# A decode step on one core: an instruction stream with two empty blocks and a hinted jump, one weight load per row of W1, a plain load of Wq, and thirty small marker loads

## The chip, the cores and the metric

The kernel runs on one core of one Trainium2 chip. Its engines are TensorE (PE, with its weight loads shown apart as PEld), VectorE (DVE), ScalarE (ACT), GpSimd (POOL) and SyncE (SP). Sixteen DMA engines move data between the chip's memory (HBM) and the core's SBUF. The metric is the device time of one execution in microseconds, as the median of the runs shown.

## The reference

One token (a row x of 1024 values) passes through two branches, and the sum of both and x is the output. Everything is bf16 at the boundary.

```
xn = layernorm(x)
q  = xn @ wq                      # 1024 x 4096: 32 heads of 128
k, v = the last 4096 rows of the cache, 4 key/value heads, each used by 8 query heads
o  = softmax(q k^T / sqrt(128)) v
A  = o @ wo                       # 4096 x 1024
y  = layernorm(xn)
B  = gelu(y @ w1 + b1) @ w2 + b2  # 1024 x 3584 and 3584 x 1024
out = x + A + B
```

Nearly all of the data is used once: wq and wo have 8 MB each, w1 and w2 7 MB each, and the two windows of the cache 4 MB each, some 40 MB in all.

## The kernel before, in words

Every engine's program is written out by hand, with semaphores between them. Two engines issue loads: SP has one queue (q1 in the profile) with all the large ones, and ACT has another (q10) with x, b1 and b2 (lines 165 to 167). In q1 the order is W1 (one load of 128 rows of 57,344 bytes), Wq in two halves, the two key loads, the two value loads, W2, and Wo in four pieces of 20, 10, 1 and 1 chunks (`WO_CHUNKS`; a chunk is 2 KB on each of 128 partitions). W2 is written over W1, so SP waits for TensorE's mark "h" (line 364); Wo is written over Wq, so SP waits for "q" (line 366). The values wait for "b1" (line 362).

Wq's second half is loaded in a special way. The even partitions get their full rows (line 229) and the odd partitions get rows that lack the last `CUT` = 1024 columns (line 230). The 64 pieces of 2 KB that are missing come by four more loads of 16 rows each (line 233) into the tile `WX`, which lies where the probabilities `Pb` will later be. TensorE needs the matching 48 values of x for these pieces, so GpSimd gathers them (line 183), TensorE turns them (line 266), VectorE normalizes them (line 286), and four more matmuls use them (line 354). The holes in `WA` are multiplied by zeros (`XNZ7`, line 292). The loads at lines 229 to 233 wait for GpSimd to have cleared the holes (lines 169 and 170).

TensorE's program runs in this order: turning x, two sums for the layer norms, b1 into seven PSUM banks (line 315), y times W1 (line 324: 8 rows of 7 matmuls, each preceded by its own weight load of one column of y), xn times Wq (line 345: 64 matmuls, then the four of line 354), eight units of sixteen transposes of the keys (line 405), the scores (line 431), the turning of h (line 438), softmax with VectorE and ScalarE, probabilities times values (line 510), and the products with W2 and Wo (line 494). At its end ScalarE copies the result out of PSUM (line 547) and SP stores it (line 549).

Within one piece of the product with Wo, TensorE waits for that piece's load alone; the last piece, of one chunk, has four matmuls.

Of the kernel before, what the change touches and what calls it, by code (L numbers as in the profile page):

```python
# [5 lines left out]
ALU = mybir.AluOpType  # L6
ACTF = mybir.ActivationFunctionType
AX = mybir.AxisListType
# [11 lines left out]
KC = D // 128  # L20
NQ = HQ * DH
WQ_CHUNKS = [4, 4]
W1_CHUNKS = [8]
W2_CHUNKS = [28]
WO_CHUNKS = [20, 10, 1, 1]
KEEP_BUSY = [[512] * 5, [], [], []]
NPAIR = HKV // 2
PB = 2 * NBLK
CUT = 1024
B1W = 256  # L30
B1N = F // B1W
XS = 2
XROWS = 48
OUTSIDE = -1e30
# [15 lines left out]
def bass_parallel_sum__sliding_block_cached__mixer_channel_mlp__decode_kernel(  # L50
# [18 lines left out]
    pe, dve, act, pool, sp = nc.tensor, nc.vector, nc.scalar, nc.gpsimd, nc.sync  # L69

    def sems(name, n):
        return [nc.alloc_semaphore(f"{name}{i}") for i in range(n)]

    s_xrow, s_b1, s_b2, s_out = (nc.alloc_semaphore(n) for n in ("s_xrow", "s_b1", "s_b2", "s_out"))
    s_wq = sems("s_wq", len(WQ_CHUNKS))
    s_ex = nc.alloc_semaphore("s_ex")
    s_w1 = sems("s_w1", len(W1_CHUNKS))
# [6 lines left out]
    DVE = Track(nc, "S_DVE")  # L84
    ACT = Track(nc, "S_ACT")
    POOL = Track(nc, "S_POOL")

    def sb(name, shape, d):
        return nc.alloc_sbuf_tensor(name, shape, d)

    f32, bf16 = dt.float32, dt.bfloat16
    identb = sb("identb", [128, 128], bf16)
    identf = sb("identf", [128, 128], f32)
# [5 lines left out]
    oneb = sb("oneb", [128, 1], bf16)  # L99
    XBR = sb("XBR", [1, 2 * D], bf16)  # L100
    XT16 = sb("XT16", [128, 16], f32)
    msx = sb("msx", [128, 8], f32)
    XNT = sb("XNT", [128, 8], f32)
    XNTb = sb("XNTb", [128, 8], bf16)
    XNZ = sb("XNZ", [128, KC * 15], bf16)
    EVEN = sb("EVEN", [128, 1], f32)
    XNZ7 = sb("XNZ7", [128, 15], bf16)
    XPR = sb("XPR", [1, XS * XROWS], bf16)
    XEZ = sb("XEZ", [XROWS, XS * 15], bf16)
    YT16 = sb("YT16", [128, 16], f32)  # L110
# [14 lines left out]
    Pb = sb("Pb", [128, PB * HQ], bf16)  # L125
# [11 lines left out]
    WA = sb("WA", [128, KC * NQ], bf16)  # L137
    WX = Pb[0:XROWS, 0:XS * CUT]
    PS = nc.alloc_psum_tensor("PS", [128, 8 * 512], f32)
# [5 lines left out]
    wq_p = A_wq.rearrange("(p r) n -> p r n", r=KC)  # L145
    wq_runs = A_wq.rearrange("(p r) n -> p (r n)", r=KC)
    wq_x = A_wq.rearrange("(s h r e k) n -> k s h e r n", s=XS, h=2, r=4, e=4)[2 * KC - 1]
    w1_p = B_w1.rearrange("(p r) n -> p r n", r=KC)
    w2_p = B_w2.rearrange("(p c) n -> p c n", c=FC)
    wo_p = A_wo.rearrange("(p j) n -> p j n", j=32)  # L150
    out_rows = out.rearrange("b s (a n) -> (b s a) n", a=4)

    C = {}

    def load_rows(dst, src, chunks, width, semaphores):
        c0 = 0
        for j, n in enumerate(chunks):
            sp.dma_start(  # L158
                dst[:, c0 * width:(c0 + n) * width].rearrange("p (c n) -> p c n", c=n),
                src[:, c0:c0 + n, :],  # L160
            ).then_inc(semaphores[j], 16)
            c0 += n
# [5 lines left out]

    POOL.mark(pool.memset(WA[:, KC * NQ - CUT:KC * NQ], 0.0))
    C["hole"] = POOL.mark(pool.memset(WX, 0.0))  # L170
    POOL.mark(pool.memset(XPR[:, :], 0.0))
    C["oneb"] = POOL.mark(pool.memset(oneb[:, :], 1.0))
# [4 lines left out]
        out=identb[:, :], in_=identb[:, :], pattern=[[-1, 128]], compare_op=ALU.not_equal,  # L177
        fill=1.0, base=0, channel_multiplier=1))
    pool.wait_ge(s_xrow, 16)
    for i in range(XS):  # L180
        at = i * 2 * 16 * 2 * KC
        dst = XPR[0:1, i * XROWS:(i + 1) * XROWS].rearrange("o (g m) -> o g m", g=3)[:, 0:3:2, :]
        C["xpr"] = POOL.mark(pool.tensor_copy(
            dst.rearrange("o h (e r) -> o h e r", e=4),
            XBR[0:1, at + 2 * KC - 1:at + 2 * 16 * 2 * KC:2 * KC].rearrange("o (h r e) -> o h e r", h=2, e=4)))
    POOL.mark(pool.memset(identf[:, :], 0.0))
# [3 lines left out]
        fill=1.0, base=0, channel_multiplier=1))  # L190
    POOL.mark(pool.memset(XNZ[:, :], 0.0))
    POOL.mark(pool.memset(XNZ7[:, :], 0.0))
    C["xnz"] = POOL.mark(pool.memset(XEZ[:, :], 0.0))
    POOL.mark(pool.memset(E4[:, :], 0.0))
# [17 lines left out]
    at = PAR[:, :].rearrange("k (m g) -> k m g", g=2)  # L212
# [12 lines left out]
    load_rows(W1, w1_p, W1_CHUNKS, F, s_w1)  # L225
    load_rows(WA, wq_p, WQ_CHUNKS[:-1], NQ, s_wq)
    sp.wait_ge(POOL.sem, C["hole"])
    c0 = (KC - WQ_CHUNKS[-1]) * NQ
    sp.dma_start(WA[0:128:2, c0:KC * NQ], wq_runs[0:128:2, c0:KC * NQ]).then_inc(s_wq[-1], 16)
    sp.dma_start(WA[1:128:2, c0:KC * NQ - CUT], wq_runs[1:128:2, c0:KC * NQ - CUT]).then_inc(s_wq[-1], 16)  # L230
    for i in range(XS):
        for h in range(2):
            sp.dma_start(WX[32 * h:32 * h + 16, i * CUT:(i + 1) * CUT], wq_x[i, h, :, :, NQ - CUT:NQ]).then_inc(s_ex, 16)

# [10 lines left out]
    def stats(src, ms, veps):  # L245
# [10 lines left out]
            out=ms[:, 5:6], in0=ms[:, 3:4], scalar=EPS, in1=ms[:, 4:5], op0=ALU.add, op1=ALU.subtract))  # L256

    xt = PS[:, 7 * 512 + 16: 7 * 512 + 24]
    pe.wait_ge(POOL.sem, C["oneb"])
    pe.wait_ge(s_xrow, 16)  # L260
    for r in range(KC):
        last = pe.matmul(xt[:, r:r + 1], lhsT=XBR[0:1, r:D:KC], rhs=oneb[0:1, :])
    xe = PS[0:XROWS, 7 * 512 + 24: 7 * 512 + 24 + XS]
    pe.wait_ge(POOL.sem, C["xpr"])
    for i in range(XS):
        last = pe.matmul(xe[:, i:i + 1], lhsT=XPR[0:1, i * XROWS:(i + 1) * XROWS], rhs=oneb[0:1, :])
    C["xt"] = PE.mark(last)
# [15 lines left out]
    DVE.mark(dve.tensor_scalar(out=XNT[:, :], in0=XT16[:, 0:8], scalar1=msx[:, 2:3], scalar2=msx[:, 7:8],  # L283
                               op0=ALU.subtract, op1=ALU.mult))
    dve.wait_ge(POOL.sem, C["xnz"])
    DVE.mark(dve.tensor_scalar(out=XEZ[:, 7:XS * 15:15], in0=xe, scalar1=msx[0:XROWS, 2:3], scalar2=msx[0:XROWS, 7:8],
                               op0=ALU.subtract, op1=ALU.mult))
    C["even"] = DVE.mark(dve.tensor_reduce(out=EVEN[:, 0:1], in_=identf[:, 0:128:2], axis=AX.X, op=ALU.add))
    dve.wait_ge(DVE.sem, DVE.cnt)
    C["xn"] = DVE.mark(dve.tensor_copy(XNTb[:, :], XNT[:, :]))  # L290
    pool.wait_ge(DVE.sem, C["xn"])
    C["xnz7"] = POOL.mark(pool.tensor_tensor(out=XNZ7[:, 7:8], in0=XNTb[:, KC - 1:KC], in1=EVEN[:, 0:1], op=ALU.mult))
    dve.wait_ge(DVE.sem, DVE.cnt)
# [10 lines left out]
    act.wait_ge(ACT.sem, ACT.cnt)  # L304
    ACT.mark(act.activation(out=EXPW[:, 0:1], in_=msy[:, 6:7], func=ACTF.Exp))
    dve.wait_ge(ACT.sem, C["std2"])
    DVE.mark(dve.reciprocal(out=msy[:, 7:8], in_=msy[:, 6:7]))
# [12 lines left out]
    for j, n in enumerate(W1_CHUNKS):  # L320
        pe.wait_ge(s_w1[j], 16)
        for _ in range(n):
            for t in range(7):
                last = pe.matmul(  # L324
                    PS[0:1, t * 512:(t + 1) * 512], lhsT=YTb[:, k:k + 1],
                    rhs=W1[:, k * F + t * 512: k * F + (t + 1) * 512],
                    start=False, stop=(k == KC - 1))
            k += 1
    C["h"] = PE.mark(last)
# [7 lines left out]
    for j, n in enumerate(WQ_CHUNKS):  # L337
        pe.wait_ge(s_wq[j], 16 if j < len(WQ_CHUNKS) - 1 else 32)
        for _ in range(n):
            for t in range(8):  # L340
                cut = k == KC - 1 and (t + 1) * 512 > NQ - CUT
                if cut:
                    pe.wait_ge(POOL.sem, C["xnz7"])
                z = XNZ7[:, 7 - t:15 - t] if cut else XNZ[:, 15 * k + 7 - t:15 * k + 15 - t]
                pe.matmul(  # L345
                    PS[0:8, 7 * 512:8 * 512], lhsT=z,
                    rhs=WA[:, k * NQ + t * 512: k * NQ + (t + 1) * 512],
                    start=(k == 0 and t == 0), stop=False)
            k += 1
    pe.wait_ge(s_ex, 32 * XS)  # L350
    for i in range(XS):
        for t in range((NQ - CUT) // 512, 8):
            at = i * CUT + t * 512 - (NQ - CUT)
            last = pe.matmul(  # L354
                PS[0:8, 7 * 512:8 * 512], lhsT=XEZ[:, 15 * i + 7 - t:15 * i + 15 - t], rhs=WX[:, at:at + 512],
                start=False, stop=(i == XS - 1 and t == 7))
    C["q"] = PE.mark(last)
# [33 lines left out]
    for u in range(NUNIT):  # L391
# [11 lines left out]
        for bb in range(16):  # L403
            o = banks[bb // 8] * 1024 + (bb % 8) * 128
            last = pe.matmul(PSb[:, o:o + 128], lhsT=KT[:, col + bb * 128: col + (bb + 1) * 128],  # L405
                             rhs=identb[:, :], is_transpose=True)
        C["ktr"][u] = PE.mark(last)
        use_act = u not in (2, 5)
        dve.wait_ge(PE.sem, C["ktr"][u])
# [134 lines left out]
    C["fin"] = PE.mark(last)  # L544

    act.wait_ge(PE.sem, C["fin"])
    C["a_out"] = ACT.mark(act.activation(out=ORow[:, :], in_=PS[:, 6 * 512:6 * 512 + 256], func=ACTF.Copy))  # L547
# [33 lines left out]
```

## Time and profile before

| what | value |
|---|---|
| time, median of 3 runs | 100.78 us (100.48, 100.78, 100.81) |
| span of the profiled execution, first to last instruction | 99.4 us |
| own time of the profiled execution | not listed apart from the three runs; median less span is 1.4 us |
| TensorE busy | 69.6 us (70% of the span), 763 matmuls, mean granted clock 0.897 |
| weight loads | 763, 42.4 us busy, beside the matmuls |
| VectorE, ScalarE, GpSimd busy | 25.8, 12.8 and 9.0 us |
| moved by DMA | 39.96 MB, mean 402 GB/s |
| queue q1 | 1832 packets, 94.1% of 16 engines' span |

The page cuts the span into 40 slices of 2.48 us and gives each engine's busy share in tenths; the DMA row is the mean share of the 16 DMA engines. A queue's share of 94.1% says that the sixteen engines were occupied with q1's packets in 94.1% of the whole span, so that a slice at 9 is a slice in which the large loads ran without a hole. A third queue, q8, is called "instruction": the fetches of program code from memory, six in this execution, of 16,384 bytes each.

### The profile page before, as it was taken

The page shows a single profiled execution, that of the slowest core. Times are in us where ns is not written, and L with a number is a line of the kernel's source. Part 1 is how long each engine was busy: PE and PEld are TensorE (multiplying, and loading weights), DVE is VectorE, ACT ScalarE, POOL GpSimd, SP SyncE. Part 2 cuts the span into 40 slices and gives each one's busy share as a digit, 9 for nine tenths or more (in the row PEclk, how much of TensorE's full clock was granted, in tenths as well). Part 3 has the DMA queues.
Part 4 walks back from the last instruction along what each step waited for, and adds up shares of the span by engine and source line. Part 5 has one row for each costly group of instructions (what it writes and reads, how often), then busy time and mean ns, then how long its engine had stood idle before and what let it go on. Part 6 is the DMA issues. An engine that isn't in the chain of part 4 may idle for free.

```text
span 99.4 us, 1681 instructions
## 1 busy us (share of the span) xinstructions
PE 69.6 (70%) x763; PEld 42.4 (43%) x763; DVE 25.8 (26%) x50; ACT 12.8 (13%) x15; POOL 9.0 (9%) x30
## 2 busy tenths in 40 slices
PE   0230860089999999999999999722799995009961
PEld 0220300023434343434399869510567894008740
DVE  0058500000000090000078921867790040000000
ACT  0500240000000050000065730005200000000001
POOL 7989100000000000000000000000000000000000
PEclk9999999999999999999999999555557999855799
DMA  9988889999999999999999999998999899699930
GB/s 347 392 372 369 370 369 485 465 422 422 422 422 422 409 402 403 441 429 442 429 429 422 429 534 416 468 485 369 392 485 425 346 445 528 287 404 437 405 143 1
DMA packets 1870, 39.96 MB, mean 402 GB/s; under 512 B 244, under 2 KB 262, under 8 KB 584
## 3 DMA queue, kind: packets, MB, share of 16 engines
q1 hardware_dynamic: 1832, 39.85, 94.1%
q8 instruction: 6, 0.10, 0.4%
q10 hardware_dynamic: 32, 0.01, 0.0%
HBM read 39.86 MB, written 0.00 MB: 401 GB/s over the span
## 4 chain that ended last, share of the span: by engine, by line
DMA 65%; PE 31%; ACT 0%; SPq 0%; issue 0%
DMA WA<-in_A_wo_dram 46%; DMA W<-in_B_w_dram 19%; PE PS L324 15%; PE PS L345 14%; PE PS L494 2%; PE PS L354 1%; ACT ORow L547 0%; SPq L158 0%
## 5 line engine op out<-in xcount | busy, mean ns | idle before, releaser
L324 PE MATMUL PS<-W,YTb 128*1 128x512 bf16 x56 | 14.4, 425 | 6.2 <-DMA W<-in_B_w_dram 6.2
L345 PE MATMUL PS<-WA,XNZ 128*8 128x512 bf16 x64 | 14.0, 379 | 0.0
L324 PEld LDWEIGHTS PS<-W,YTb 128*1 128x1 bf16 x56 | 5.1, 91 | 16.0 <-issue 10.3
L510 PE MATMUL PS<-KV,Pb 128*32 128x256 bf16 x64 | 10.0, 333 | 1.2 <-ACT Pb L471 1.2
L494 PE MATMUL PS<-WA,OT 128*32 128x256 bf16 x128 | 5.6, 345 | 7.1 <-DMA WA<-in_A_wo_dram 7.1
L345 PEld LDWEIGHTS PS<-WA,XNZ 128*8 128x8 bf16 x64 | 5.6, 88 | 8.2
L510 PEld LDWEIGHTS PS<-KV,Pb 128*32 128x32 bf16 x64 | 7.4, 118 | 3.9 <-ACT Pb L471 1.7
L494 PEld LDWEIGHTS PS<-WA,OT 128*32 128x32 bf16 x128 | 4.5, 123 | 8.4 <-issue 6.3
L333 DVE CAST ROW<-PS 1x2048 bf16<-1x2048 f32 x1 | 2.3, 2279 | 22.2 <-PE PS L324 22.2
L417 ACT ACTIVATE KV<-PS 128x1024 bf16<-128x1024 bf16 x6 | 5.8, 1021 | 16.1 <-PE PS L405 16.1
L405 PE MATMUL PS<-identb,KV 128*128 128x128 bf16 x128 | 7.5, 219 | 0.0
L405 PEld LDWEIGHTS PS<-identb,KV 128*128 128x128 bf16 x128 | 7.2, 98 | 0.5 <-issue 0.4
L412 DVE COPY KV<-PS 128x1024 bf16<-128x1024 bf16 x10 | 6.4, 686 | 1.1 <-PE PS L405 1.1
L331 ACT ACTIVATE ROW<-PS 1x1536 bf16<-1x1536 f32 x1 | 1.4, 1440 | 21.2 <-PE PS L324 21.2
L359 DVE CAST Q<-PS 8x512 bf16<-8x512 f32 x1 | 0.7, 678 | 12.5 <-PE PS L354 12.5
L475 DVE TENSOR_REDUCE SUMP<-Pb 128x32 f32<-128x2048 bf16 x1 | 3.6, 3566 | 1.2 <-ACT Pb L471 1.2
L547 ACT ACTIVATE ORow<-PS 128x256 bf16<-128x256 f32 x1 | 0.4, 384 | 27.0 <-PE PS L494 27.0
L299 PE MATMUL PS<-YT,onesf 128*128 128x16 f32 x2 | 0.6, 383 | 4.2 <-DVE YT L297 4.2
L431 PEld LDWEIGHTS PS<-QT,KV 128*128 128x128 bf16 x128 | 3.3, 96 | 0.4 <-issue 0.4
L494 PE MATMUL PS<-W,GT 128*32 128x256 bf16 x112 | 3.4, 273 | 0.0
L431 PE MATMUL PS<-QT,KV 128*128 128x16 bf16 x128 | 3.4, 169 | 0.0
L442 DVE TENSOR_REDUCE MXP<-PS 128x32 f32<-128x2048 f32 x1 | 2.3, 2292 | 3.9 <-PE PS L431 3.9
(104 smaller groups left out, 48.8 us busy)
## 6 DMA issues: line engine op xcount, KB each, us to landing
W<-in_B_w_dram SPq DMA_DIRECT2D x2, 7168.0 KB, 31.0
WA<-in_A_wo_dram SPq DMA_DIRECT2D x1, 5120.0 KB, 40.0
WA<-in_A_wq_dram SPq DMA_DIRECT2D x1, 4096.0 KB, 28.6
KV<-in_A_k_cache_dram SPq DMA_DIRECT2D x2, 2048.0 KB, 40.2
KV<-in_A_v_cache_dram SPq DMA_DIRECT2D x2, 2048.0 KB, 43.6
WA<-in_A_wo_dram SPq DMA_DIRECT2D x1, 2560.0 KB, 45.7
WA<-in_A_wq_dram SPq DMA_DIRECT2D x1, 2048.0 KB, 31.2
WA<-in_A_wq_dram SPq DMA_DIRECT2D x1, 1920.0 KB, 36.7
```

Source lines behind the costliest of these rows:

```text
L324: last = pe.matmul(PS[0:1, t * 512:(t + 1) * 512], lhsT=YTb[:, k:k + 1], rhs=W1[:, k * F + t * 512: k * F + (t + 1) * 512], start=False, s ...
L331: C["a_hrow"] = ACT.mark(act.activation(out=Hrow[:, 0:1536], in_=PS[0:1, 0:1536], func=ACTF.Copy))
L333: C["d_hrow"] = DVE.mark(dve.tensor_copy(Hrow[:, 1536:F], PS[0:1, 1536:F]))
L345: pe.matmul(PS[0:8, 7 * 512:8 * 512], lhsT=z, rhs=WA[:, k * NQ + t * 512: k * NQ + (t + 1) * 512], start=(k == 0 and t == 0), stop=False)
L405: last = pe.matmul(PSb[:, o:o + 128], lhsT=KT[:, col + bb * 128: col + (bb + 1) * 128], rhs=identb[:, :], is_transpose=True)
L412: C["dkt"][u] = DVE.mark(dve.tensor_copy(KT[:, col + 1024 * s: col + 1024 * (s + 1)], PSb[:, bk * 1024:(bk + 1) * 1024]))
L417: C["akt"][u] = ACT.mark(act.activation(out=KT[:, col + 1024: col + 2048], in_=PSb[:, bk * 1024:(bk + 1) * 1024], func=ACTF.Copy))
L431: last = pe.matmul(PS[:, o:o + 2 * REP], lhsT=KT[:, (i * PB + b) * 128:(i * PB + b + 1) * 128], rhs=QT[:, i * 2 * REP:(i + 1) * 2 * REP], ...
L442: C["mxp"] = DVE.mark(dve.tensor_reduce(out=MXP[:, :], in_=PS[:, 0:2048].rearrange("p (b n) -> p n b", b=PB), axis=AX.X, op=ALU.max))
L475: C["sump"] = DVE.mark(dve.tensor_reduce(out=SUMP[:, :], in_=Pb[:, :].rearrange("p (b n) -> p n b", b=PB), axis=AX.X, op=ALU.add))
L494: ins = pe.matmul(acc(a), lhsT=vec[:, c:c + 32], rhs=weights[:, c * D + a * 256: c * D + (a + 1) * 256], start=False, stop=(c == stop_at))
L510: last = pe.matmul(PS[0:32, 4 * 512:4 * 512 + NPAIR * DH], lhsT=Pb[:, b * HQ:(b + 1) * HQ], rhs=V4[:, :, b, :], start=(b == 0), stop=(b == ...
```

## The change

The changed kernel does four things.

- Wq is loaded by two plain loads of 128 full rows. `CUT`, `WX`, `XPR`, `XEZ`, `XNZ7` and all that served them (three memsets, the gathers, six matmuls, three operations of VectorE, one of GpSimd, four loads, SP's wait) go.
- In the product with W1, the first matmul of each row loads the column of y, and the other six are issued as matmuls without a weight load (`again`).
- TensorE's first instruction is a branch-prefetch hint. After the fourth unit of key transposes its program has a branch that is never taken, a hinted jump to `L_far`, and then three alignments to 256 instructions, so that the third and the fourth block of 256 hold nothing that runs.
- ScalarE issues a series of fifteen small loads twice (`marks`): load n takes n rows of 2n values of x (4n bytes) to n partitions. The first series stands behind the operation of line 305, the second ahead of the final copy, and ScalarE waits for all of the first before the second and for all of the second before the copy.

```diff
+JUMP_AT = 363
-CUT = 1024
-XS = 2
-XROWS = 48
...
+    MK = sb("MK", [128, 240], bf16)
...
+    def again(out, lhsT, rhs, start, stop):
+        return pe.add_instruction(mybir.InstMatmult(
+            name=nc.get_next_instruction_name(), engine=pe.engine, ins=[pe.lower_ap(rhs), pe.lower_ap(lhsT)], outs=[pe.lower_ap(out)],
+            start_tensor_calc=start, stop_tensor_calc=stop, ldweights=False, tile_size=(128, 32), tile_position=(0, 0)))
...
+    def marks():
+        for n in range(1, 16):
+            act.dma_start(MK[0:n, n * (n - 1):n * (n + 1)],
+                          A_x.rearrange("b s (k n) -> (b s k) n", n=64)[0:n, 0:2 * n]).then_inc(s_mark, 16)
+
+    never = pe.alloc_register("never")
+    done = [72]
+
+    def count(n):
+        done[0] += n
+        if done[0] - n < JUMP_AT <= done[0]:
+            pe.br_lt(never, 0, on_true="L_gap", on_false="L_go")
+            nc.switch_bb("L_go", parent=None)
+            pe.br("L_far").branch_hint(C["hint"])
+            nc.switch_bb("L_gap", parent=None)
+            for _ in range(3):
+                pe.nop(hint="gap")
+                pe.addr_align(256, offset=0, max_nops=0)
+            pe.br("L_far")
+            nc.switch_bb("L_far", parent=None)
...
-    load_rows(WA, wq_p, WQ_CHUNKS[:-1], NQ, s_wq)
-    sp.wait_ge(POOL.sem, C["hole"])
-    c0 = (KC - WQ_CHUNKS[-1]) * NQ
-    sp.dma_start(WA[0:128:2, c0:KC * NQ], wq_runs[0:128:2, c0:KC * NQ]).then_inc(s_wq[-1], 16)
-    sp.dma_start(WA[1:128:2, c0:KC * NQ - CUT], wq_runs[1:128:2, c0:KC * NQ - CUT]).then_inc(s_wq[-1], 16)
-    for i in range(XS):
-        for h in range(2):
-            sp.dma_start(WX[32 * h:32 * h + 16, i * CUT:(i + 1) * CUT], wq_x[i, h, :, :, NQ - CUT:NQ]).then_inc(s_ex, 16)
+    load_rows(WA, wq_p, WQ_CHUNKS, NQ, s_wq)
...
+    C["hint"] = pe.mark_branch_hint_location()
+    pe.reg_mov(never, 0)
...
     ACT.mark(act.activation(out=EXPW[:, 0:1], in_=msy[:, 6:7], func=ACTF.Exp))
+    marks()
...
             for t in range(7):
-                last = pe.matmul(
+                put = pe.matmul if t == 0 else again
+                last = put(
                     PS[0:1, t * 512:(t + 1) * 512], lhsT=YTb[:, k:k + 1],
...
+            count(8)
...
+    act.wait_ge(s_mark, 16 * 15)
+    marks()
+    act.wait_ge(s_mark, 2 * 16 * 15)
     act.wait_ge(PE.sem, C["fin"])
```

More of the change, by code (lines that the diff above doesn't have):

```diff
@@ L72, in sems @@
         return [nc.alloc_semaphore(f"{name}{i}") for i in range(n)]
+    s_mark = nc.alloc_semaphore("s_mark")
     s_xrow, s_b1, s_b2, s_out = (nc.alloc_semaphore(n) for n in ("s_xrow", "s_b1", "s_b2", "s_out"))
     s_wq = sems("s_wq", len(WQ_CHUNKS))
-    s_ex = nc.alloc_semaphore("s_ex")
     s_w1 = sems("s_w1", len(W1_CHUNKS))
@@ L104, in bass_parallel_sum__sliding_block_cached__mixer_channel_mlp__decode_kernel @@
     XNTb = sb("XNTb", [128, 8], bf16)
+    MK = sb("MK", [128, 240], bf16)
     XNZ = sb("XNZ", [128, KC * 15], bf16)
[L106 to L109, printed above, removed]
     YT16 = sb("YT16", [128, 16], f32)
@@ L137, in bass_parallel_sum__sliding_block_cached__mixer_channel_mlp__decode_kernel @@
     WA = sb("WA", [128, KC * NQ], bf16)
-    WX = Pb[0:XROWS, 0:XS * CUT]
     PS = nc.alloc_psum_tensor("PS", [128, 8 * 512], f32)
@@ L145, in bass_parallel_sum__sliding_block_cached__mixer_channel_mlp__decode_kernel @@
     wq_p = A_wq.rearrange("(p r) n -> p r n", r=KC)
-    wq_runs = A_wq.rearrange("(p r) n -> p (r n)", r=KC)
-    wq_x = A_wq.rearrange("(s h r e k) n -> k s h e r n", s=XS, h=2, r=4, e=4)[2 * KC - 1]
     w1_p = B_w1.rearrange("(p r) n -> p r n", r=KC)
@@ L167, in bass_parallel_sum__sliding_block_cached__mixer_channel_mlp__decode_kernel @@
     act.dma_start(XBR[:, D:2 * D], b2_row).then_inc(s_b2, 16)
-    POOL.mark(pool.memset(WA[:, KC * NQ - CUT:KC * NQ], 0.0))
-    C["hole"] = POOL.mark(pool.memset(WX, 0.0))
-    POOL.mark(pool.memset(XPR[:, :], 0.0))
     C["oneb"] = POOL.mark(pool.memset(oneb[:, :], 1.0))
@@ L178, in bass_parallel_sum__sliding_block_cached__mixer_channel_mlp__decode_kernel @@
         fill=1.0, base=0, channel_multiplier=1))
-    pool.wait_ge(s_xrow, 16)
-    for i in range(XS):
[L181 to L185, printed above, removed]
     POOL.mark(pool.memset(identf[:, :], 0.0))
@@ L190, in bass_parallel_sum__sliding_block_cached__mixer_channel_mlp__decode_kernel @@
         fill=1.0, base=0, channel_multiplier=1))
-    POOL.mark(pool.memset(XNZ[:, :], 0.0))
-    POOL.mark(pool.memset(XNZ7[:, :], 0.0))
-    C["xnz"] = POOL.mark(pool.memset(XEZ[:, :], 0.0))
+    C["xnz"] = POOL.mark(pool.memset(XNZ[:, :], 0.0))
     POOL.mark(pool.memset(E4[:, :], 0.0))
@@ L225, in bass_parallel_sum__sliding_block_cached__mixer_channel_mlp__decode_kernel @@
     load_rows(W1, w1_p, W1_CHUNKS, F, s_w1)
-    load_rows(WA, wq_p, WQ_CHUNKS[:-1], NQ, s_wq)
-    sp.wait_ge(POOL.sem, C["hole"])
-    c0 = (KC - WQ_CHUNKS[-1]) * NQ
-    sp.dma_start(WA[0:128:2, c0:KC * NQ], wq_runs[0:128:2, c0:KC * NQ]).then_inc(s_wq[-1], 16)
-    sp.dma_start(WA[1:128:2, c0:KC * NQ - CUT], wq_runs[1:128:2, c0:KC * NQ - CUT]).then_inc(s_wq[-1], 16)
-    for i in range(XS):
-        for h in range(2):
-            sp.dma_start(WX[32 * h:32 * h + 16, i * CUT:(i + 1) * CUT], wq_x[i, h, :, :, NQ - CUT:NQ]).then_inc(s_ex, 16)
+    load_rows(WA, wq_p, WQ_CHUNKS, NQ, s_wq)
     def load_cache(dst, cache, semaphores):
@@ L262, in bass_parallel_sum__sliding_block_cached__mixer_channel_mlp__decode_kernel @@
         last = pe.matmul(xt[:, r:r + 1], lhsT=XBR[0:1, r:D:KC], rhs=oneb[0:1, :])
[L263 to L266, printed above, removed]
     C["xt"] = PE.mark(last)
@@ L284, in bass_parallel_sum__sliding_block_cached__mixer_channel_mlp__decode_kernel @@
                                op0=ALU.subtract, op1=ALU.mult))
+    dve.wait_ge(DVE.sem, DVE.cnt)
+    DVE.mark(dve.tensor_copy(XNTb[:, :], XNT[:, :]))
     dve.wait_ge(POOL.sem, C["xnz"])
[L286 to L292, printed above, removed]
     dve.wait_ge(DVE.sem, DVE.cnt)
@@ L337, in bass_parallel_sum__sliding_block_cached__mixer_channel_mlp__decode_kernel @@
     for j, n in enumerate(WQ_CHUNKS):
-        pe.wait_ge(s_wq[j], 16 if j < len(WQ_CHUNKS) - 1 else 32)
+        pe.wait_ge(s_wq[j], 16)
         for _ in range(n):
             for t in range(8):
[L341 to L346, printed above, removed]
+                last = pe.matmul(
+                    PS[0:8, 7 * 512:8 * 512], lhsT=XNZ[:, 15 * k + 7 - t:15 * k + 15 - t],
                     rhs=WA[:, k * NQ + t * 512: k * NQ + (t + 1) * 512],
-                    start=(k == 0 and t == 0), stop=False)
+                    start=(k == 0 and t == 0), stop=(k == KC - 1 and t == 7))
+                count(2)
             k += 1
[L350 to L356, printed above, removed]
     C["q"] = PE.mark(last)
@@ L407, in bass_parallel_sum__sliding_block_cached__mixer_channel_mlp__decode_kernel @@
         C["ktr"][u] = PE.mark(last)
+        count(32)
         use_act = u not in (2, 5)
```

## The prediction

> **What bounds the kernel now.** I read the chain of waits first, then the DMA queues, then the busy time by stage over the last microseconds, and last each load's sixteen completion writes.
>
> ```profile
> by line: DMA WA<-in_A_wo_dram 46.0%; DMA W<-in_B_w_dram 19.5%; PE PS L324 14.5%; PE PS L345 13.9%; PE PS L494 1.6%; PE PS L354 1.0%; ACT ORow L547 0.4%; SPq L158 0.3%; issue 0.3%
> ...
> 20.28 14.43 PE PS L324 x56
> 34.71 13.81 PE PS L345 x64
> 48.52 0.97 PE PS L354 x4
> 49.49 0.02 issue
> 49.51 0.34 SPq L158
> 49.85 0.04 issue
> 49.89 45.70 DMA WA<-in_A_wo_dram
> 95.59 0.04 issue
> 95.64 1.61 PE PS L494 x48
> ```
>
> The chain shows TensorE for 29 us between W1's load and Wo's. That is misleading: Wo is issued at 49.5 us because "q" is ready then, but it stands behind the values and W2 in a queue that never runs empty.
>
> ```profile
> DMA  9988889999999999999999999998999899699930
> ...
> q1 hardware_dynamic: 1832, 39.85, 94.1%
> q8 instruction: 6, 0.10, 0.4%
> ```
>
> 94.1% of 99.4 us is 93.5 us of packets on each of 16 engines, from 1.8 us to 96.4 us. So DMA is the bound from end to end: 39.85 MB at the 27.1 GB/s of one engine (a 57,344-byte packet takes 2.116 us) are 91.9 us. TensorE waits for Wo's first piece, and this is its slack:
>
> ```profile
> PE PS L494 <- DMA WA<-in_A_wo_dram: 7.1, 2, 6.2
> ```
>
> The end is set by the **slowest of the sixteen engines**. The table by stage gives PE, weight load, DVE, ACT, POOL, then the granted clock, the DMA share and GB/s:
>
> ```profile
> 94.50:95.00 0.50, 0.17 (x1) 0.00 (x0) 0.00 (x0) 0.00 (x0) 0.00 (x0) 1.00 0.47 176
> 95.00:95.50 0.50, 0.00 (x0) 0.00 (x0) 0.00 (x0) 0.00 (x0) 0.00 (x0) 1.00 0.59 225
> 95.50:96.00 0.50, 0.36 (x16) 0.36 (x20) 0.00 (x0) 0.00 (x0) 0.00 (x0) 1.00 0.52 197
> 96.00:96.50 0.50, 0.50 (x28) 0.49 (x20) 0.00 (x0) 0.00 (x0) 0.00 (x0) 1.00 0.12 45
> ```
>
> About half of the engines are still loading for 1.5 us after the other half have finished. The completion writes (us, sorted, from the trace) tell which work made them late:
>
> ```
> Wq, 1st half    all 16 within 29.32 to 29.88
> Wq, even rows   15 from 38.73 to 39.22, one at 40.83
> values, 2nd     10 from 58.31 to 58.80, six from 59.78 to 60.41
> W2              8 from 75.26 to 75.75, eight from 76.72 to 77.36
> Wo, 1st piece   7 from 87.41 to 87.87, nine from 88.85 to 89.48
> Wo, last piece  7 from 94.81 to 95.31; 96.25 96.32 96.42 96.56; 96.57 96.58 96.65 96.71 96.87
> ```
>
> The instruction fetches start at 36.59, 56.24, 64.49, 75.15, 85.86 and 96.75 us, and after each of the first five one more engine is late. Each fetch hit a *different* engine, by 1.55 us (39.27 expected, 40.83 seen): about 1.0 us in which it moves no data, and 0.5 us by which its next packet is stretched (a 30,720-byte packet takes 1.687 instead of 1.138 us). Four others are late since the pieces of line 233, whose completion writes come from four engines only: 16 pieces of 2 KB each, four in 0.337 us, about 1.3 us. So nine engines are late, and the last completion at 96.87 us is the first fetch's engine, which had also been the last of all before it. Four matmuls, the copy and the store then take 2.5 us.
>
> **The change part by part.**
>
> *Wq plain.* The 64 cut pieces come from all engines alike (4 rows each, 8 KB) and go to four. Undone, four engines get 24 KB less and twelve, the five late ones among them, 8 KB more: 8192 / 27.1 GB/s = **+0.30 us** on each fetch engine. This is the surest term. The operations that go (GpSimd's 1.8 and 0.95 us memsets, line 286, the 0.97 us of line 354) lie beside the loads of W1 and Wq: worth nothing, for the queue is full without them. SP no longer waits 2.3 us at line 229; the loads ahead of it last until 29 us, so nothing.
>
> *One weight load per row.* Line 324 needs 14.43 / 56 = 258 ns per matmul and line 345 216 ns. If the 48 matmuls without loads go at 216 ns, TensorE gains 48 x 42 ns = 2.0 us. Bounds: nothing to 2.0 us, and a loss if such a matmul were slower. Both are hidden, since W2 is issued at 34.7 us and its turn in the queue comes at 59 us. On the time: 0.
>
> *Jump and hint.* [...] Engines without a fetch end within 0.50 us of one another (94.81 to 95.31), and before the latest of them was hit. After: the same (0) or an earlier one (down to -0.30). I take **-0.1**. [...]
>
> The row for code fetches is 16 KB in 0.93 us, ahead of any need. [...]
>
> *Markers.* Load n has n rows, so 2 x 120 = 240 data packets and as many completion writes, at most 30 of each on one engine, 15 on the mean. (The b1 load of 14 rows made 14 packets and 14 writes.) Nearest rows: 9 ns for a 4-byte packet, 27 ns for 512 bytes, 17 ns for a completion write between the pieces of line 233. Lower bound 0: the b1 engines show no visible delay at W1's end. Upper: 30 x 44 = 1.32 us. I take 15 x 15 ns = **+0.2**, nearest to the 4-byte row. ScalarE issues fifteen at 0.43 to 0.85 us each: 6 to 13 us, from 13.6 us (next needed at 34.7) and from 70.2 us (next needed at 97.3), so hidden. The waits: behind the second stands only the final copy. A small load advances by one packet per packet of q1 (b2 needed from 2.7 to 13.7 us), so 30 steps from 70 us end near 95 us, within the loads. Cost 0; cover about 1 us.
>
> **Sum.** Last completion 96.87 + 0.30 - 0.1 + 0.2 = 97.3 us; span 99.4 + 0.4 = 99.8 us; with the 1.4 us between span and median, **101.2 us**. Bounds of the three terms: 100.8 to 102.4.
>
> **Rivals.**
>
> *Same engine twice.* If a block is fetched twice (hint early, pushed out, fetched again) or two blocks share an engine, that engine is late twice. For: only five distinct engines are known. Against: all five did differ. Price: 0.6 us (16 KB at packet speed) to 1.55 us more, 101.8 to 102.8; it decides once one engine has two fetches before 96 us.
>
> [...]
>
> *Fewer or cheaper fetches.* If a fetch costs only the 1.0 us, or code comes before the loads start, the last is 96.3 us: 100.2. Against: all five measured about 1.55.
>
> [...]
>
> **Numbers.** Forecast 0.55, twice 0.17, not slower 0.18, cheaper 0.10. About 0.3% (0.3 us) is what a measurement here can tell. Of the forecast's 0.55, 0.43 is over +0.3 us; with the second case: slower 0.60. Same: 0.12 + 0.17 = 0.29. Faster: 0.11. Range 100.6 to 102.5: it leaves out the cheaper fetches and the upper part of the second case.
>
> **What would show it.** No late engines behind Wq's end except fetched ones; the late ones 0.3 us later; the number of code packets five to seven; L324's time near 12.4 us without moving the end. Wrong would be: an end not set by Wo's last completion, a fetch-free engine that is last (markers too dear), or ScalarE's copy waiting for markers.

## The result and the profile after

The changed kernel takes 101.46 us (median of 4 runs, 101.1 to 101.56), the kernel before, run beside it, 100.65 us (4 runs, 100.48 to 100.81, the three known before and one more): a ratio of 1.0073, with a 95% interval from 1.0045 to 1.0102. The forecast was 101.2 us, slower. The profiled execution took 101.56 us with a span of 100.3 us; it is the longest of the four. One run each of a2 and a4 below was over 1.5% above the fastest of its kernel and is left out of the medians and ratios.

The chain of waits of the changed kernel, its last part (start, duration, what):

```profile
48.62 41.72 DMA WA<-in_A_wo_dram
90.34 0.14 issue
90.48 4.46 PE PS L482 x73
94.94 1.74 PE PS L531 x5
96.67 1.43 PE PS L482 x45
98.11 0.02 issue
98.13 0.02 ACTq L537
98.15 0.05 issue
98.20 0.38 ACT ORow L538
```

Before, the chain went from Wo's load straight into the last 48 matmuls. Now it leaves the load at 90.34 us, when Wo's *first* piece had landed, and goes through TensorE: 73 of that piece's 80 matmuls, the five of line 531 that keep TensorE busy and that no output uses, and 45 of the last 48. ACTq L537 is ScalarE's wait for the markers, 0.02 us, with 0.05 us of issue behind it: no marker was still to come, but the wait itself stands between the last matmul and the copy (98.11 to 98.20 us, 0.09; before 97.24 to 97.26).

The DMA row and the queues of the changed kernel:

```profile
DMA  9798889799999999999999999988989979989910
...
q1 hardware_dynamic: 1736, 39.85, 93.3%
q8 instruction: 6, 0.10, 0.4%
q10 hardware_dynamic: 512, 0.02, 0.3%
```

The row is still full from end to end. There are 96 packets less in q1 (the 64 cut pieces of Wq and 32 completion writes), again six code fetches, and 480 packets more in q10: 240 marker rows, each with a completion write. They move 0.02 MB.

TensorE's wait for Wo's first piece, which was 6.2 us, and the last microseconds by stage (PE, weight load, DVE, ACT, POOL, clock, DMA share, GB/s):

```profile
PE PS L482 <- DMA WA<-in_A_wo_dram: 8.9, 1, 8.9
```

```profile
95.00:95.50 0.50, 0.50 (x2) 0.15 (x1) 0.00 (x0) 0.00 (x0) 0.00 (x0) 0.50 0.71 254
95.50:96.00 0.50, 0.50 (x3) 0.17 (x2) 0.00 (x0) 0.00 (x0) 0.00 (x0) 0.50 0.34 131
96.00:96.50 0.50, 0.50 (x6) 0.24 (x8) 0.00 (x0) 0.00 (x0) 0.00 (x0) 0.66 0.32 123
96.50:97.00 0.50, 0.50 (x24) 0.49 (x22) 0.00 (x0) 0.00 (x0) 0.00 (x0) 1.00 0.12 45
97.00:97.50 0.50, 0.50 (x30) 0.50 (x21) 0.00 (x0) 0.00 (x0) 0.00 (x0) 1.00 0.01 4
```

Two things differ from before. The DMA share shows about a third of the engines still loading from 95.5 to 96.5 us, where it was about half until 96.0 us, and single ones until after 97 us. And TensorE, which before stood idle at 95.0 to 95.5 us, is busy throughout, at a granted clock of 0.50 until 96.34 us.

The completion writes of Wo's last piece, sorted, and their mean, tell it engine by engine. They are from the traces of the two kernels:

```
before   94.81 to 95.31 (7)   96.25 to 96.87 (9)            last 96.87   mean 95.92
after    95.40 to 95.88 (10)  96.48  96.96 to 97.10 (4)     last 97.59   mean 96.20
```

The code fetches of the changed kernel start at 44.26, 55.37, 62.67, 73.29, 83.10 and 95.01 us. None comes near the hint at the start of TensorE's program (0.9 us), and TensorE shows no stall at the jump: around it, behind the fourth unit of transposes, the matmuls start 56 ns apart.

Both readings of the sum can be made here: the last completion is 97.59 - 96.87 = 0.72 us later (forecast 0.43), and from there to the end of the span it is 2.7 us instead of 2.5.

### The profile page after: what moved, and what is told of

It is laid out like the page before. It is cut to its first block, busy times and chain, and to the rows that moved or that the text cites. A ratio compares the mean times of both kernels' runs of the same rounds, so it can differ in the third digit from the quotient of the medians.

```text
span 100.3 us, 1642 instructions
## 1 busy us (share of the span) xinstructions
PE 68.3 (68%) x757; PEld 38.0 (38%) x709; DVE 25.3 (25%) x48; ACT 12.8 (13%) x15; POOL 5.6 (6%) x22
## 3 DMA queue, kind: packets, MB, share of 16 engines
q1 hardware_dynamic: 1736, 39.85, 93.3%
## 4 chain that ended last, share of the span: by engine, by line
DMA 61%; PE 36%; issue 0%; ACT 0%; ACTq 0%
DMA WA<-in_A_wo_dram 42%; DMA W<-in_B_w_dram 19%; PE PS L338 14%; PE PS L147 12%; PE PS L482 6%; PE PS L320 2%; PE PS L531 2%; ACT ORow L538 0%; ACTq L537 0%
## 5 line engine op out<-in xcount | busy, mean ns | idle before, releaser
L147 PE MATMUL PS<-W,YTb 128*1 128x512 bf16 x48 | 13.4, 420 | 0.0
L482 PE MATMUL PS<-WA,OT 128*32 128x256 bf16 x128 | 6.1, 365 | 8.9 <-DMA WA<-in_A_wo_dram 8.9
L498 PE MATMUL PS<-KV,Pb 128*32 128x256 bf16 x64 | 8.6, 305 | 1.2 <-ACT Pb L459 1.2
L320 PE MATMUL PS<-W,YTb 128*1 128x512 bf16 x8 | 3.5, 437 | 7.6 <-DMA W<-in_B_w_dram 7.6
L320 PEld LDWEIGHTS PS<-W,YTb 128*1 128x1 bf16 x8 | 0.7, 89 | 20.4 <-issue 20.4
L498 PEld LDWEIGHTS PS<-KV,Pb 128*32 128x32 bf16 x64 | 6.8, 108 | 3.2 <-ACT Pb L459 1.7
L310 PE MATMUL PS<-KV,oneb 1*1 1x512 bf16 x7 | 3.1, 622 | 1.4 <-DMA KV<-in_B_b_dram 1.4
```

The lines of the kernel that those rows point to most:

```text
L147: return pe.add_instruction(mybir.InstMatmult(name=nc.get_next_instruction_name(), engine=pe.engine, ins=[pe.lower_ap(rhs), pe.lower_ap(lh ...
L310: last = pe.matmul(PS[0:1, t * 512:(t + 1) * 512], lhsT=oneb[64:65, :], rhs=B1R[:, 2 * t:2 * t + 2, :], start=True, stop=False)
L320: last = put(PS[0:1, t * 512:(t + 1) * 512], lhsT=YTb[:, k:k + 1], rhs=W1[:, k * F + t * 512: k * F + (t + 1) * 512], start=False, stop=(k ...
L482: ins = pe.matmul(acc(a), lhsT=vec[:, c:c + 32], rhs=weights[:, c * D + a * 256: c * D + (a + 1) * 256], start=False, stop=(c == stop_at))
L498: last = pe.matmul(PS[0:32, 4 * 512:4 * 512 + NPAIR * DH], lhsT=Pb[:, b * HQ:(b + 1) * HQ], rhs=V4[:, :, b, :], start=(b == 0), stop=(b == ...
```

## The experiments

**Theory** at this point: a plain Wq costs 0.3 us, the jump and the single weight load nothing, and the rest is markers, which cost the engine that ends last more than the mean. **Rivals**: the jump brings another fetch onto a late engine; or the marker loads cost through ScalarE, the wait ahead of the copy or the low clock at the end, and not through the DMA engines.

### Part by part

Four kernels: the changed one without markers (a1), the changed one without the jump (a2), and the kernel before with plain Wq alone (b1) or with markers alone (b2).

a1:

```diff
-    marks()
...
-    act.wait_ge(s_mark, 16 * 15)
-    marks()
-    act.wait_ge(s_mark, 2 * 16 * 15)
```

> The changed kernel without its thirty marker loads and the two waits on them. Theory D (the end is the slowest DMA engine; in the changed kernel the engine of the first fetch was already 0.4 us late at the end of Wq, from markers): the last completion of Wo falls from 97.59 us to 97.0 to 97.2 us, the time from 101.46 to about 101.0 us. Rival P (the end is TensorE's, which ran the five extra matmuls after Wo's first piece at half clock, 2.06 us instead of 1.24): no more than 0.15 us is gained. Rival J (the jump and its hint cost the time): 101.4 us.

a2:

```diff
-JUMP_AT = 363
+JUMP_AT = 10 ** 9
...
-    C["hint"] = pe.mark_branch_hint_location()
-    pe.reg_mov(never, 0)
```

> The changed kernel without hint, jump and empty blocks; markers, plain Wq and the single weight loads stay. Theory D: code blocks three to seven are fetched again in place of five to nine, on other engines; every fetched engine still has 0.30 us more data and its share of markers, so the last completion is at 97.0 to 97.4 us and the time 101.0 to 101.3 us. Rival P: 101.4 us, as the wait for Wo and so the clock stay the same. Rival J: the whole of the 0.8 us beside the 0.3 us of plain Wq goes, 100.9 us.

b1 takes over from the change the plain load and the removal of everything that served the cut pieces:

```diff
-    load_rows(WA, wq_p, WQ_CHUNKS[:-1], NQ, s_wq)
-    sp.wait_ge(POOL.sem, C["hole"])
...
+    load_rows(WA, wq_p, WQ_CHUNKS, NQ, s_wq)
```

> The kernel before with Wq loaded in two plain loads and nothing else changed. Theory D: 8 KB more on each of the twelve engines, last completion 96.87 + 0.30 = 97.17 us, only the five fetched engines late behind the rest (not nine), time 100.65 + 0.30 = 100.95 us. Rivals P and J: 100.65 us, no change.

b2:

```diff
+    marks()
     dve.wait_ge(ACT.sem, C["std2"])
...
+    act.wait_ge(s_mark, 16 * 15)
+    marks()
+    act.wait_ge(s_mark, 2 * 16 * 15)
     act.wait_ge(PE.sem, C["fin"])
```

> The kernel before with the two series of markers and ScalarE's waits, and nothing else changed. Theory D: markers cost 15 to 25 ns each on the engine that carries them; the four engines with the pieces of line 233 end at 96.25 to 96.56 us without markers and get up to 30 of them, so they end at 96.8 to 97.3 us and become the last: time 100.9 to 101.1 us. Rivals P and J: 100.65 us, no change.

Measured, with the last and the mean of the sixteen final completions in the profiled execution:

```
                       us (median)   ratio to before [95%]      last    mean
b1 plain Wq alone      100.98        1.0041 [1.0027, 1.0055]    97.15   95.85
b2 markers alone       101.11        1.0053 [1.0040, 1.0066]    97.23   96.18
a1 without markers     100.91        1.0028 [1.0017, 1.0039]    96.99   95.92
a2 without the jump    101.30        1.0055 [1.0035, 1.0074]    97.39   96.26
```

Plain Wq costs 0.41%. In b1 eleven engines end by 95.66 us and only five later than 96.6 us, so the four engines of line 233 were late because of their pieces, as the prediction read it; the last is at 97.15 us, where 96.87 + 0.30 = 97.17 was forecast. Markers cost 0.53% alone, and 0.45% as the difference between the changed kernel and a1 (its interval, from the two intervals, is about 0.3% to either side). The jump's difference has both signs: a1 against b1 (which differ by the single weight load as well) is 0.13% lower, the changed kernel against a2 is 0.18% higher; neither can be told from nothing.

The chain of a1 ends as that of the kernel before does:

```profile
48.19 47.53 DMA WA<-in_A_wo_dram
95.71 0.04 issue
95.75 1.60 PE PS L481 x48
97.36 0.02 issue
97.38 0.38 ACT ORow L534
```

So without the markers TensorE is not at the end of the chain; Wo's load is.

### The single weight load and the jump alone

b3 is the kernel before with one weight load per row, b4 the same with the hint and the jump as well; both keep the special load of Wq and have no markers.

```diff
-                last = pe.matmul(
+                put = pe.matmul if t == 0 else again
+                last = put(
```

> The kernel before with one weight load per row of W1 and nothing else. Theory D: TensorE's product with W1 may get shorter, the end does not move, 100.65 us (plus or minus 0.15, as 48 instructions fewer move the block borders and so the moment of a fetch). Rival: the product was on the chain, and its saving is seen at the end, 99 us or less.

```diff
+JUMP_AT = 363
...
+    C["hint"] = pe.mark_branch_hint_location()
+    pe.reg_mov(never, 0)
...
+            count(8)
...
+                count(2)
...
+        count(32)
```

> The kernel before with one weight load per row of W1 and the hinted jump over two empty blocks; the special loads of Wq stay and there are no markers. Theory D: jump and weight loads are worth what they were beside plain Wq (100.91 against 100.98), 100.5 to 100.7 us, unless one of the fetches now hits one of the four engines that carry the pieces of line 233, which makes it 0.9 to 1.2 us more, 101.5 to 101.9 us. Rival J (jump and hint cost time by themselves): 101.0 us or more without such an engine.

Measured: b3 100.9 us, 1.001 [0.9986, 1.0034]; b4 100.85 us, 0.9996 [0.9981, 1.0010]. Both are no change. But TensorE did not become faster at the rows of W1 either. These are parts of the changed kernel's chain (line 320 is the first matmul of a row, line 147 the six others):

```profile
20.48 0.59 PE PS L320
21.07 2.56 PE PS L147 x6
23.62 0.43 PE PS L320
24.05 1.66 PE PS L147 x6
25.71 0.22 PE PS L320
25.93 1.29 PE PS L147 x6
...
34.78 13.83 PE PS L338 x64
```

From the third row on, a row takes 0.22 + 1.29 = 1.51 us, 216 ns for each of seven matmuls; the first row takes twice that. In the kernel before, the busy time of line 324 by stage (columns: length, then PE, weight load, DVE and ACT, clock, DMA share, GB/s) shows the same slow start:

```profile
22.00:24.00 2.00, 2.00 (x6) 0.58 (x5) 0.00 (x0) 0.00 (x0) 1.00 0.99 426
...
30.00:32.00 2.00, 2.00 (x11) 0.80 (x10) 0.00 (x0) 0.00 (x0) 1.00 1.21 524
```

Six matmuls lie in or across a stretch of 2 us at the start and eleven in one later, with a weight load beside each of them. So the 258 ns per matmul of the prediction was a mean over a slow start and 216 ns, and the excess of 42 ns was not the weight loads' price. The product ends at 34.78 us, before it was 34.71.

The slow start is the clock, though the clock column has 1.00 there. The traces have no clock record before the one that sets 1.00, at 24.73 us in the kernel before and at 24.66 us in the changed one, and the column prints 1.00 for a time without a record. Up to that moment the matmuls of W1 follow one another at 427 ns, from then on at 216 ns. So it is in all fourteen traces: the step from 427 to 216 ns lies within 0.13 us of the first clock record, which comes between 23.17 us (a1, c1) and 26.73 us (c2). The product takes 13.6 us where the record comes at 23.17 us and 15.2 us where it comes at 26.73 us. That the clock stood at half before is read from these steps, as no record says it.

### Which engines are hit

To see which engine was late, two kernels carry three series of fifteen tiny loads (of 1 to 15 rows) in SP's queue, so that an engine can be known by the first load of a series that reaches it: m1 is the kernel before with them, m2 the changed kernel with them in place of ScalarE's. The diff is m2's; m1 has a semaphore for each series, and SP waits for the first series ahead of the third.

```diff
+    def series(i):
+        for n in range(1, 16):
+            sp.dma_start(MK[0:n, 120 * i + n * (n - 1) // 2:120 * i + n * (n + 1) // 2],
+                         A_x.rearrange("b s (k n) -> (b s k) n", n=64)[0:n, 0:n]).then_inc(s_mark, 16)
```

> The kernel before with three series of fifteen tiny loads in SP's own queue: behind the values, behind W2 and behind Wo's first piece. Load n has n rows, so a DMA engine shows by the first of the series that it carries which one it is, and stands in the queue's order, so that its lateness at that point can be read with its name. Theory D: at the first series the four engines with the pieces of line 233 are late and so are the engines of the fetches so far, all different; 0.3 to 0.9 us is added to the time by 45 loads (up to 45 x 18 ns = 0.8 us on one engine). Rival E (a code fetch always goes by one engine and the lateness moves by other means): one name for all fetches.

> The changed kernel with the same three series in SP's queue in place of ScalarE's two. Theory D: five late engines with five names; if the engine follows the block of code that is fetched, the names differ from those of the kernel before by the two blocks that are left out, at least for the later fetches; if it follows the order of fetches, the names are the same. The time is 101.0 to 101.5 us. Rival E: one name.

Both times were far from what I expected: 106.95 us and 105.78 us (one run each). SP needed 13 to 25 us to issue one series (ScalarE 5 to 6 us in the changed kernel), and 45 tiny loads in q1 made the last engine 6.6 to 7.9 us later than the first at the end, though inside a series the packets are only 12 ns apart. What they wait for was not settled; the kernels are of use for their map alone.

The map: ahead of the first series, the engines that were late in m1 are those that loads of 1, 2, 3 and 4 rows reach first, and the sixth and the seventh. In m2 they are the sixth and the seventh alone. So the pieces of line 233 fell on the first four engines in m1, and the first two fetches on the sixth and seventh in both kernels. Ahead of the second series the tenth and eleventh are added, in both. The later ones are less certain, since the series themselves move the engines apart. So skipping two blocks did not choose other engines, as far as the first four fetches go: they fell on the same four in both.

The loads of line 233 have 16 rows, which their source gives as four groups of four. In the trace of the kernel before each of them has four completion writes, where each large load has sixteen. By the map the four are the first four engines: they are late in m1, and none of them in m2, which has no such loads.

Where the markers lie can be worked out on one assumption, that a load of n rows gives one row to each of the first n engines. In the trace of the changed kernel the 240 rows have 240 completion writes, and in c1 below loads of four rows move exactly four engines; that the larger loads reach the same engines again is assumed. On that, each of the first four carries between 24 and 30 of the thirty rows, the sixth 20, the seventh 18, the tenth 12 and the eleventh 10. The two engines that are fetched from first, and were last already, carry more than the mean of 15.

### Where the markers fall, and how many

c1 and c2 keep thirty marker loads, ScalarE's issues and its waits, and change the rows of each; c3 has the first series alone.

c1, and c2 with 15 in place of 4:

```diff
-            act.dma_start(MK[0:n, n * (n - 1):n * (n + 1)],
-                          A_x.rearrange("b s (k n) -> (b s k) n", n=64)[0:n, 0:2 * n]).then_inc(s_mark, 16)
+            act.dma_start(MK[0:4, n * (n - 1):n * (n + 1)],
+                          A_x.rearrange("b s (k n) -> (b s k) n", n=64)[0:4, 0:2 * n]).then_inc(s_mark, 16)
```

> The changed kernel, but each of the thirty marker loads takes four rows instead of n: the same number of loads, waits and issues, and half of the packets (120 instead of 240). Theory A (a marker costs the engine that carries it, some 18 to 30 ns for each data packet and its completion write, and only an engine that was also fetched from sets the end): loads of four rows fall on the four engines that had the pieces of line 233 and that no fetch hit; those become 30 x 18 to 30 ns = 0.5 to 0.9 us late, end by 96.5 us, and nobody waits for them. Time as without markers: 100.9 us (100.8 to 101.05). Theory B (the loads themselves cost, by ScalarE's issues, the wait ahead of the copy or the queue): as the changed kernel, 101.4 to 101.5.

> The changed kernel, but each marker load takes fifteen rows: again thirty loads, with 450 packets, so that all engines but one carry 30 of them. Theory A: the fetched engines carry 30 instead of about 20 (the first ones) or 10 (the later ones), which is 10 x 18 to 30 ns more at the end: 101.65 to 101.75 us, and the sixteen last completions later by 15 x 18 = 0.27 us on the mean. Theory B (the loads cost, not where they fall): 101.4 to 101.5.

c3:

```diff
     act.wait_ge(s_mark, 16 * 15)
-    marks()
-    act.wait_ge(s_mark, 2 * 16 * 15)
```

> The changed kernel with the first series of fifteen markers alone; ScalarE still waits for it ahead of the final copy. Theory A: half of the packets, half of the cost, wherever in the stream they are: 101.15 us (101.05 to 101.25). Rival, the second series or the wait for it at the end is what costs: 100.9.

Measured, beside a1 and the changed kernel (the third column is what the first two fetched engines carry by that assumption):

```
                  us       ratio to before [95%]      markers   last    mean    first 11 engines to end
a1 none           100.91   1.0028 [1.0017, 1.0039]    0         96.99   95.92   95.31 to 95.65
c1 30 x 4 rows    101.04   1.0039 [1.0026, 1.0051]    0         97.21   96.13   95.37 to 95.70 (7), 96.09 to 96.29 (4)
c3 15 x n rows    101.21   1.0056 [1.0041, 1.0071]    10, 9     97.33   96.05   95.36 to 95.86
changed kernel    101.46   1.0073 [1.0045, 1.0102]    20, 18    97.59   96.20   95.40 to 96.48
c2 30 x 15 rows   101.83   1.0116 [1.0097, 1.0134]    30        97.96   96.63   95.52 to 96.85
```

The queue's packets show that loads alone do not count. c1:

```profile
q10 hardware_dynamic: 272, 0.02, 0.2%
```

c2:

```profile
q10 hardware_dynamic: 932, 0.03, 0.6%
```

With the same thirty loads and waits the time goes from 101.04 to 101.83 us, with the rows on the engines that end last: 0.79 us for 30 rows, 26 ns each. In c1 four engines, and exactly four, move to 96.09 to 96.29 us, about 0.7 us behind the other seven (95.37 to 95.70): 30 markers at some 23 ns each. Nobody waits for them, since the last engine, at 97.21 us, is later still. Theory A is borne out, and theory B, that a load costs wherever it falls, is not. The last completion goes from 96.99 us (none) over 97.33 (10) and 97.59 (20) to 97.96 (30): 0.97 us for 30 markers, 32 ns each. These are single executions. c2 came out 0.1 us above its expectation, and not all of it is the engine's own rows: the first engine to end in c2 is at 95.52 us instead of 95.31, and in c1 the last engine, which carries none, is 0.2 us later than in a1. This common part was not taken apart, beyond the 0.07 us that ScalarE's wait adds to the time of every kernel with markers. A third reading, a price by the total number of rows, is not excluded by the times alone: c1 and c3 have 120 rows each, and their 0.17 us of difference lies within their intervals. Against it stand the four engines of c1, which alone carry its rows and alone fall back behind the others.

### The matmuls that keep TensorE busy

a4 is the changed kernel without the five matmuls of line 531, whose result no output uses.

```diff
-KEEP_BUSY = [[512] * 5, [], [], []]
+KEEP_BUSY = [[], [], [], []]
```

> The changed kernel without the five matmuls that keep TensorE busy between the first and the second piece of Wo (work that no output uses). Theory: in the changed kernel's profile these matmuls ran at a low clock until 96.67 us and pushed the 45 matmuls behind them to 98.11 us, though the last load landed at 97.59; without them the last four matmuls follow the load by 0.15 us, so that 0.1 to 0.35 us go: 101.1 to 101.35. Rival: without them the clock falls further or stays at half, and the matmuls of the pieces take as long as the ones left out: no change, 101.45 or more.

Measured: 102.52 us (101.31 to 102.73), ratio 1.0152 [1.0109, 1.0195]. The rival held, and more than held: it became slower by about 1 us. The end of its chain:

```profile
48.85 47.40 DMA WA<-in_A_wo_dram
96.24 0.04 issue
96.29 2.78 PE PS L482 x40
```

And its busy time by stage:

```profile
95.00:96.00 1.00, 0.00 (x0) 0.00 (x0) 0.00 (x0) 0.00 (x0) 0.00 (x0) 0.50 0.45 166
96.00:97.00 1.00, 0.71 (x16) 0.55 (x20) 0.00 (x0) 0.00 (x0) 0.00 (x0) 0.50 0.21 80
97.00:98.00 1.00, 1.00 (x28) 0.72 (x24) 0.00 (x0) 0.00 (x0) 0.00 (x0) 0.50 0.06 16
```

Without them TensorE idles at 95 us and goes into the last matmuls at a clock of 0.50: 40 of the last 48 stand on the chain and take 2.78 us, where in the changed kernel 45 of the 48 take 1.43 us at 1.00. In a4's trace the clock is at 0.50 from 85.75 us to 99.40 us, in the changed kernel's from 86.11 to 96.34 us. So the five matmuls do not cost the changed kernel 0.35 us. Though they ran at half clock and TensorE reached the last pieces late, with them the clock is back at 1.00 for the matmuls that decide. Not every execution of a4 loses it: one of the six took 101.31 us, at a mean clock of 0.898, where the others had 0.865 to 0.883.

No version beat the kernel before by more than its measurement: b4 is the lowest, at 0.9996.

## Why the prediction was right, and where it was not

The time lay in the range, and the direction was right, by the cause that the prediction named. The change itself was 0.81 us and the forecast one 0.4 us: the plain Wq came as forecast, the markers cost more than twice their term, and the gain of the jump did not come.

**Bound and end.** Right. The queue stayed full, and the end moved with the last of sixteen engines in the tables above; in b2, a2 and the changed kernel TensorE added a little of its own (see the tail below), and in a4 the clock did.

**Wq plain, +0.30 us, "the surest term".** Right: 0.41% [0.27, 0.55] in b1, and the last completion within 0.02 us of the forecast.

**One weight load per row, 0.** Right on the time (b3: 1.001 [0.9986, 1.0034]), for another reason than the one given. TensorE's 2.0 us are not hidden, they do not exist: 258 ns was a mean over two unlike parts, 427 ns ahead of the rise of the clock and 216 ns behind it, and both hold with and without the weight loads. The sign that was named for it, a product of near 12.4 us, did not come: the product took 14.30 us (34.78 - 20.48), before 14.43.

**Jump and hint, -0.1 us.** No effect that can be told from nothing (b4 against b3 0.14% lower, a1 against b1 0.13% lower, the changed kernel against a2 0.18% higher). No run shows the -0.1 us. What the traces show is six fetches in either kernel, the first at 44.26 us where it was at 36.59, and none near the hint at 0.9 us. They do not say at which instruction a fetch begins, which block it brings or what the hint does: the five to seven code packets of the forecast, and the blocks and block borders in what was expected of a2 and b3, are my estimate. The argument about *which* engine is hit had the wrong idea behind it: the first four fetches fell on the same engines in both kernels (m1, m2), so there was no new engine to win. The sixth, at 95.01 us, left no sixth engine as late as the five: the one that ended at 96.48 us was 0.5 us behind already at Wo's first piece (89.02, the ten ahead of it 87.92 to 88.52).

No wait of TensorE for code was seen: in the kernel before, the changed kernel, a1 and b4 each of its idle times over 0.1 us (the longest 8.9 us in the changed kernel, for Wo's first piece) ends with another engine's mark or a load's landing, none with code. The load that the same DMA engine carries comes later for it: in a1 the first fetched engine lands its share of the keys at 45.84 us, the next one at 44.53, and it keeps these 1.3 us to the end. No stall was seen at the hinted jump, where the matmuls start 56 ns apart; a jump without a hint was not run.

**Markers, +0.2 us.** This is the step that failed, by its size: "I take 15 x 15 ns". Measured were 0.45 to 0.53%, about 0.5 us. The mean over engines was well estimated (96.20 - 95.92 = 0.28 us in the changed kernel, 0.26 us in b2, or 18 ns for a row with its completion write). But the prediction had itself said that the slowest engine sets the end, and then put the mean on it. With the 20 rows that the sixth engine carries and 18 ns, the term is 0.36 us, which is what b2's last completion shows (97.23 against 96.87). With the 0.07 us of ScalarE's wait and 0.12 us of TensorE's (both below) that is the 0.55 us by which b2's profiled span is longer (99.90 against 99.35). In the changed kernel against a1 the last completion moves by 0.60 us; there the slowest of four executions stands against the fastest of seven, and the medians differ by 0.55 us in all. The upper bound, 30 x 44 ns = 1.32 us, was on the safe side of c2's 0.97 us.

**The tail of 2.5 us.** Taken as fixed, and 0.2 us too short here. 0.07 us of it is ScalarE's wait (0.09 instead of 0.02 us between the last matmul and the copy), which every kernel with markers has. The rest lies between the last landing and the last matmul's end: 0.37 us before and in a1, b1, c1, c2 and 0.36 in c3, but 0.49 to 0.52 us in b2, a2 and the changed kernel. In these three TensorE is not yet through with the earlier pieces when the last one lands. In the kernel before the last four matmuls start 0.05 us behind the last landing; in b2 and a2 they start 0.18 and 0.19 us behind it, right after the 44 matmuls of the second and third piece, which take 1.22 us from the second piece on. That piece landed only 1.08 and 1.07 us ahead of the last one there, 1.28 us before. In the changed kernel it landed 1.24 us ahead, but the last of the five matmuls of line 531 ran until 96.76 us, beside the first ones of the second piece, and the last matmul starts 0.21 us behind the last landing.

**Rivals.** No engine shows the price of two fetches; the fetches did not become cheaper (from Wq's end to the first keys the last engine goes from 40.00 to 46.46 us in the changed kernel, the first from 39.25 to 44.15: 1.56 us more). ScalarE's wait ahead of the copy, forecast at nothing, cost the 0.07 us above. The range, 100.6 to 102.5 us, held the time with room to spare.

**A label.** The row "Wq, even rows" of the prediction's completion writes is the load of the odd rows (packets of 30,720 bytes); that of the even rows landed from 34.18 to 34.72 us. Nothing was worked out from the label.

## What to carry to other kernels

In these kernels sixteen DMA engines work with hardly a hole (93.3% of the changed kernel's span), and there a load's price was what it added to the engine that ended last, not to the mean: 0.60 us on the last completion for the markers (changed kernel against a1), where the mean moved by 0.28 us. So list the completion writes of the last load, find out which engines are late and why, and count the rows of each small load engine by engine. Thirty marker loads of four rows fell on four engines, none of them the last to end, and gave 101.04 us against 100.91 without markers (c1, a1); thirty of fifteen rows, on the engines that end last too, gave 101.83 us (c2). And divide a stretch's time by its count only after seeing whether it runs evenly (W1's 258 ns were 427 and then 216), and ask of a clock column whether there is a record behind it (1.00 stood there ahead of the first record, at 24.73 us).

## What the runs showed that was not expected

- A marker row of 4 to 60 bytes shows as a packet of 9 to 11 ns, but with its completion write it made its engine 18 to 32 ns later: 18 by the mean over engines, 23 by c1's four engines, 32 by c2's last completion.
- Forty-five tiny loads in the queue that carries the large loads cost 5 to 6 us (m1, m2), thirty in ScalarE's queue about 0.5 us. The cause is open.
- Five matmuls whose result is thrown away are worth about 1 us at the end of this kernel in five of six executions of a4, by the clock of the matmuls behind them (40 of them in 2.78 us at 0.50 without the five, 45 in 1.43 us at 1.00 with them).
- After a wait of 7.6 us for W1, the first row of seven matmuls took 3.15 us instead of 1.51 us, at half clock by their steps of 427 ns, while the profile's column, without a record for that time, gives 1.00.
